# Seven of sixteen blocks of a re-read V half kept in a constant's buffer and in spare PSUM columns, with the first q blocks written by VectorE

## The chip, the cores and the metric

One NeuronCore of a Trainium2 chip runs the whole kernel as one launch. TensorE (PE) multiplies, VectorE (DVE), ScalarE (ACT) and GpSimd (POOL) do the rest, SyncE (SP) issues the loads, and sixteen DMA engines move the bytes from the chip's main memory into on-chip memory (SBUF); matmul results land in PSUM, eight banks of 512 float32 columns per partition. The metric is the device time of one execution in microseconds (us). The kernel before took 178.01 us (median of 3 runs, 177.15 to 178.4).

## The reference

Four tokens (batch 4, one position, width 512) go through attention, a gated MLP, the same attention and the same MLP again, each with a layer norm before it and a residual after it. Attention looks at the last W = 2048 of 8192 cached positions; 32 query heads share 8 key/value heads.

```python
x = x + attn(layernorm(x)); x = x + mlp(layernorm(x))   # twice, with the same weights and caches
# attn: q = x @ wq; p = softmax(q k^T * Dh**-0.5) over 2048 keys; o = p v; o @ wo
# mlp:  (sigmoid(x @ w_gate) * (x @ w_up)) @ w_down,   512 -> 1792 -> 512
```

In bfloat16 one pass over the keys is 16 MB (4 batches, 8 heads, 2048 keys, 128 values) and one over the values as much again. wq and wo are 4 MB each, the three MLP matrices 1.75 MB each.

## The kernel before, in words

**Stages.** The first q projection, attention over heads 0 to 7 (`attn_first`), the MLP (`glu`, k = 0), the second q projection (`q_second`), attention over heads 7 to 0 (`attn_second`, whose steps are called 2.0 to 2.7; step 2.0 is head 7), the MLP again (k = 1).

**Memory and loads.** SBUF is one `arena` of 50 slots of 4 KB per partition and a smaller tensor `side` of scratch. All K blocks stay in the arena from the first pass to the second. V does not fit, so it is loaded twice, but for a few blocks: some stay in the arena, and some wait in PSUM banks that are idle between the passes. VectorE puts them there with `transpose` (`stash`, line 578, and `stash_half`, line 600) and takes them back (line 593 in `load_stash`, line 606 in `unstash_half`). A "tile" is two slots: for head h and batch pair bp, 64 partitions for each of two batches, 32 keys on each, so that a half tile (one slot) is 16 key blocks of 128 values. Tile (6, 0) is kept by half: its second half stays where it was (`KEPT`), its first half is loaded again as `("Vh", 0, 6, 0, 1)`, 512 KB.

**Places.** Between the passes the weights of the first MLP and of the second q projection are loaded into half tiles. Each is given its place by name in the source: `Y`, `Z` and `GA` are the tiles of V (7, 0), (7, 1) and (6, 0), `WQ` is the first tile of wq, `SP` is `side`. `homes` holds the place of each load, `hfree` the halves that are free by then, `give` frees one by hand, `done` frees what was read for the last time. A load waits for the last reader of its place; SP issues the loads in the written order, so a load that waits holds back all behind it (line 401 issues every load).

**Order of work.** Each operation is recorded with what it reads and writes (`P.op`). A planner (`_schedule`) then runs through all of them with estimated durations and gives each engine a fixed order; `_assign_sync` puts in the semaphore waits. From the first MLP on, TensorE's order is the written order (`P.chain = True`).

**The second q projection and the first two scores.** wq is used in two halves: half 1 feeds heads 4 to 7 and is multiplied first (`q_mms(1, 1, ...)`, line 828), `q_turn` transposes the result on VectorE (line 840, named qt) and scales it into `qh` (line 844, qc). For each score step TensorE then spreads one head's q into a block form with four matmuls against shifted identities (`qx`, line 875) and ScalarE copies that to `qbd` (`qe`, line 880). The score (`softmax_unit`) is first four matmuls that write the mask (M, line 905) and then sixteen with q and K (S, line 916). In step 2.0 the matmuls of wq block (1, 0) stand between M and S (argument `between`). After the scores VectorE takes the maximum (mx, line 929). Each score frees its K slots for loads of V:

```python
qx(0)
score(0, lambda: q_mms(1, 0, OBS[1], (1,)))
qx(1)
score(1)
turn(0)
```

`permo` (128 x 512, bfloat16) is a constant, a permutation that VectorE writes at the start (line 705). TensorE reads it once per step of the first attention (`pm`, line 1024) and then not again until step 2.7.

Of the kernel before, what the change touches and what calls it, by code (L numbers as in the profile page):

```python
# [6 lines left out]
F32 = mybir.dt.float32  # L7
# [271 lines left out]
def build(nc, A_x, A_k, A_v, A_wq, A_wo, B_wg, B_wu, B_wd, out, cfg=None):  # L279
# [45 lines left out]
    with es:  # L325
# [90 lines left out]

        homes = {}
# [71 lines left out]
        def load_half(name, src, rate, size, where_):  # L489
            left[name] = 1  # L490
            homes[name] = [where_]
            on_free[name] = lambda s: hfree.add(s)

            def emit(s):
                dma(str(name), slot_ap(s)[:, 0:size], src, w=stok(s, size), rate=rate)
            loads.append((name, emit))
# [25 lines left out]
        def load_wq(k):  # L522
# [3 lines left out]
            else:  # L526
                for i in (1, 0):
                    for c in range(i, NC):
                        load_half(("wq", c, k, i), wq_d[:, c, i * SLOT:(i + 1) * SLOT], "bw_4k", SLOT,
                                  (((Y, 0), (Y, 1), (WQ, 1), (WQ, 0)), (None, (WQ, 0), (GA, 0), (SP, 0)))[i][c])  # L530
# [23 lines left out]
        def load_glu(k):  # L554
            for nm, src, two in (("wg", wg_d, wg_p), ("wu", wu_d, wu_p)):
                if k == 0:
                    for c in range(NC):
                        load_half((nm, c, k), src[:, c, :], "bw_3k", F,
                                  (((WQ, 0), (GA, 0), (SP, 0), (Y, 0)), ((Y, 1), (Z, 0), (WQ, 0), (GA, 0)))[nm == "wu"][c])
# [3 lines left out]
            for n, (a, b) in enumerate(bounds_of(k)):  # L563
                if k == 0:
                    load_half(("wd", a, k), wd_d[:, a:b, :].rearrange("p k n -> p (k n)"), "bw_4k", (b - a) * D,
                              ((SP, 0), (Y, 0), (Y, 1), (Z, 0))[n])
# [42 lines left out]
        def load_v(h, bp, k, n_use):  # L609
            name = ("V", h, bp, k)  # L610
            tiles = {(HKV - 2, 0): ((GA, 0),), (HKV - 3, 1): ((Y, 0), (Y, 1))}.get((h, bp)) if k else None
            if tiles is not None:
                halves[h, bp] = []
                for n, tile in enumerate(tiles):
                    half = ("Vh", n, h, bp, k)
                    load_half(half, pair_d(A_v, h, bp)[:, :, n * SLOT:(n + 1) * SLOT], "bw_4k", SLOT, tile)
                    halves[h, bp].append((half, 0))
                if len(tiles) == 1:
                    halves[h, bp].append((KEPT, 0))
                return  # L620
# [5 lines left out]
        def keep_half(s):  # L626
            hfree.add(s)
            where[KEPT] = s + 1
            left[KEPT] = 2
        on_free[GA] = keep_half  # L630
# [205 lines left out]
        def q_turn(k, i, qb, buf=None, toks=(("e", 0), ("e", 1)), after=()):  # L836
# [4 lines left out]
                 r=[("qrow", i)], w=toks, banks=(qb,), after=after)  # L841
            qi = qh[:, i * 64:(i + 1) * 64]
# [14 lines left out]
        def q_second(variance):  # L857
# [3 lines left out]
            q_mms(1, 1, WB, (2, 3))  # L861
            q_mms(1, 0, OBS[1], (0,))
            fresh.append(q_turn(1, 1, WB))
# [28 lines left out]
        late = {}  # L892

        def softmax_unit(tag, hk, wait=False, q=True, between=None):
# [3 lines left out]
            bank, pt = {HKV: (OBS[0], 2), HKV + 1: (WB, 3)}.get(u, (SB[k2], k2))  # L898
# [3 lines left out]
            def e_m(pe):  # L902
                last = None
                for gi in range(4):
                    last = pe.matmul(ps[32 * gi:32 * gi + 32, bank, :], msk_s[:, :],  # L905
                                     msk_m[:, :].unsqueeze(1).broadcast_to([128, 256, 2]), start=True, stop=False)
                return last

            def e_s(pe):
# [664 lines left out]
```

## Time and profile before

| what | value |
|---|---|
| median of 3 runs (range) | 178.01 us (177.15 to 178.4) |
| the profiled execution's own time | 177.0 us |
| its span, first to last instruction | 175.3 us |
| busy: PE, DVE, ACT, POOL | 105.7, 104.4, 32.7, 22.2 us |
| bytes by DMA | 70.00 MB, mean 399 GB/s |
| first attention ends, first MLP (last wo matmul to the residual) | 104.8 us, 118.5 us |
| second attention, from the first score to the residual | 124.6 to 163.0 us |

The page is one execution. "Busy" is time in which an engine executed; the idle time of an engine that does not bound the kernel costs nothing. The DMA rows are the engines' busy share in tenths and the GB/s moved, in 40 slices of 4.38 us. An "issue" is SP's instruction that starts a load; a load is done ("lands") when all sixteen engines have finished their shares. The clock that the profile grants to TensorE is 1.00 until 157 us and 0.50 after.

### The profile page before, as it was taken

Reading aid. Unit: us, or ns where it says so; the run is one execution under the profiler, and the core shown is the slowest. Engines: PE = TensorE matmul, PEld = TensorE weight load, DVE = VectorE, ACT = ScalarE, POOL = GpSimd, SP = SyncE. Lnnn points to the kernel's source line nnn. Section 1 sums busy time; section 2 is a strip of 40 time slices with the busy share of each in tenths; the row PEclk is TensorE's granted clock in tenths of the full one; section 3 lists DMA queues with packets and bytes.
Section 4 is the critical chain, followed back from the end, with each engine's and each line's share of the span. In section 5 each row is a group of like instructions: output and inputs, shape, how many; then the busy total and the mean of one; then the engine's idle time right before and its main releaser. Section 6 shows DMA issues by size and latency. Waiting matters only on the chain.

```text
span 175.3 us, 3927 instructions
## 1 busy us (share of the span) xinstructions
PE 105.7 (60%) x1661; PEld 54.7 (31%) x1661; DVE 104.4 (60%) x257; ACT 32.7 (19%) x87; POOL 22.2 (13%) x90
## 2 busy tenths in 40 slices
PE   0536246259566273661765456547977999776673
PEld 0203112014334041340445452142322444445321
DVE  6307997994957738378322381316299999751351
ACT  2002031322303003021030000100143455430011
POOL 6100010101101001010010000000011453442000
PEclk9999999999999999999999999999999999995555
DMA  5999999999999999999999999999999999999980
GB/s 188 426 426 426 426 419 424 408 421 423 419 419 412 420 424 426 421 405 427 419 419 415 415 400 407 402 410 403 394 413 404 423 419 424 421 416 423 419 344 25
DMA packets 12226, 70.00 MB, mean 399 GB/s; under 512 B 1320, under 2 KB 1328, under 8 KB 6064
## 3 DMA queue, kind: packets, MB, share of 16 engines
q1 hardware_dynamic: 12200, 69.74, 97.1%
q8 instruction: 13, 0.21, 0.5%
q14 instruction: 5, 0.04, 0.1%
q10 hardware_dynamic: 8, 0.00, 0.0%
HBM read 69.73 MB, written 0.00 MB: 398 GB/s over the span
## 4 chain that ended last, share of the span: by engine, by line
DMA 52%; DVE 24%; PE 19%; issue 2%; SPq 1%; ACT 0%; DVEq 0%
DMA arena<-in_A_v_cache_dram 20%; DMA arena<-in_B_w_down_dram 18%; DVE arena L887 12%; DMA arena<-in_A_wq_dram 10%; PE ps L916 8%; DMA arena<-in_B_w_gate_dram 5%; DVE small L929 3%; PE ps L905 3%; PE ps L1088 2%; DVE small L933 1%; DVE arena L593 1%; PE ps L1006 1%; DVE side L937 1%; PE ps L828 1%; DVE small L941 1%
## 5 line engine op out<-in xcount | busy, mean ns | idle before, releaser
L887 DVE STREAM_TRANSPOSE arena<-arena 128x1024 f32<-128x1024 f32 x32 | 37.0, 1205 | 0.1
L1006 PE MATMUL ps<-side,arena 128*128 128x8 bf16 x576 | 18.2, 168 | 14.1 <-DMA arena<-in_A_v_cache_dram 14.0
L916 PE MATMUL ps<-arena,side 128*32 128x512 bf16 x256 | 25.0, 524 | 0.1
L1006 PEld LDWEIGHTS ps<-side,arena 128*128 128x128 bf16 x576 | 16.7, 104 | 20.5 <-DMA arena<-in_A_v_cache_dram 18.8
L929 DVE TENSOR_REDUCE small<-ps 128x1 f32<-128x512 f32 x16 | 10.8, 676 | 17.6 <-PE ps L916 17.5
L944 ACT ACTIVATE side<-ps,small 128x512 bf16<-128x512 f32 x16 | 11.0, 687 | 36.8 <-PE ps L1024 18.3
L905 PE MATMUL ps<-small,msk_s 128*32 128x512 bf16 x64 | 8.4, 512 | 13.9 <-DVE arena L887 13.1
L880 ACT CAST side<-ps 128x256 bf16<-128x256 f32 x16 | 5.9, 370 | 34.4 <-PE ps L916 25.4
L959 ACT CAST side<-ps 128x512 bf16<-128x512 f32 x16 | 9.4, 586 | 10.8 <-PE ps L957 10.8
L916 PEld LDWEIGHTS ps<-arena,side 128*32 128x32 bf16 x256 | 8.2, 119 | 10.0 <-issue 7.2
L973 POOL CAST small<-small 128x1 bf16<-128x1 f32 x9 | 1.7, 188 | 76.1 <-ACT side L944 76.1
L957 PE MATMUL ps<-side,perm 128*128 128x512 bf16 x16 | 7.9, 494 | 5.2 <-ACT side L944 5.2
L828 PE MATMUL ps<-arena,xn 128*4 128x512 bf16 x60 | 7.5, 572 | 3.9 <-DMA arena<-in_A_wq_dram 3.6
L784 ACT ACTIVATE small<-ps 128x4 f32<-128x4 f32 x4 | 0.7, 174 | 48.1 <-PE ps L780 48.1
L1379 PE MATMUL ps<-arena,xn 128*4 128x448 bf16 x60 | 7.2, 549 | 3.3 <-DMA arena<-in_B_w_up_dram 1.5
L964 DVE STREAM_TRANSPOSE side<-side 128x256 f32<-128x256 f32 x16 | 6.9, 433 | 2.0 <-ACT side L959 1.8
L875 PE MATMUL ps<-side,eyew 32*128 32x64 bf16 x64 | 5.6, 217 | 3.4 <-ACT side L880 2.4
L1088 PE MATMUL ps<-arena,side 128*32 128x512 bf16 x112 | 7.3, 381 | 0.2 <-DVE small L941 0.2
L1014 DVE TENSOR_TENSOR onb<-ps,rinv 128x16 bf16<-128x16 f32 x9 | 1.7, 185 | 9.0 <-PE ps L1006 8.8
L905 PEld LDWEIGHTS ps<-small,msk_s 128*32 128x32 bf16 x64 | 1.7, 97 | 16.8 <-DVE arena L887 15.4
L1388 DVE STREAM_TRANSPOSE side<-ps 128x448 f32<-128x448 f32 x4 | 2.6, 650 | 7.3 <-PE ps L1379 7.3
L840 DVE STREAM_TRANSPOSE side<-ps 128x512 f32<-128x512 f32 x3 | 2.1, 716 | 7.9 <-PE ps L828 7.8
(123 smaller groups left out, 137.8 us busy)
## 6 DMA issues: line engine op xcount, KB each, us to landing
arena<-in_A_v_cache_dram SPq DMA_DIRECT2D x27, 1024.0 KB, 18.8
arena<-in_A_k_cache_dram SPq DMA_DIRECT2D x16, 1024.0 KB, 24.9
arena<-in_A_wq_dram SPq DMA_DIRECT2D x4, 1024.0 KB, 7.8
arena<-in_A_wo_dram SPq DMA_DIRECT2D x3, 1024.0 KB, 26.5
arena<-in_A_wq_dram SPq DMA_DIRECT2D x6, 512.0 KB, 6.3
arena<-in_B_w_up_dram SPq DMA_DIRECT2D x4, 448.0 KB, 6.1
arena<-in_B_w_gate_dram SPq DMA_DIRECT2D x2, 896.0 KB, 21.7
arena<-in_B_w_up_dram SPq DMA_DIRECT2D x2, 896.0 KB, 23.9
```

What stands on the lines that cost most here:

```text
L828: last = pe.matmul(ps[32 * hh:32 * hh + NB, qb, :], xn[:, c * NB:(c + 1) * NB], src[:, o + hh * 512:o + (hh + 1) * 512], start=(c == 0), s ...
L887: P.op("vector", "T%d_%d" % (h, t), c_dve(1024), lambda v, v32=v32: v.transpose(v32, v32), r=[("slot", 4 * h + t)], w=[("slot", 4 * h + t)])
L905: last = pe.matmul(ps[32 * gi:32 * gi + 32, bank, :], msk_s[:, :], msk_m[:, :].unsqueeze(1).broadcast_to([128, 256, 2]), start=True, stop= ...
L916: last = pe.matmul(ps[32 * gi:32 * gi + 32, bank, :], qbd[:, q0:q0 + 32], kt[:, cp // 2, cp % 2, jh * NJ:(jh + 1) * NJ, :], start=False, s ...
L929: lambda v: v.tensor_reduce(nmax[:, k2:k2 + 1], ps[:, bank, :], AXX, ALU.max),
L944: lambda a: a.activation(prow[:, :].rearrange("p (m x t) -> p m x t", x=32, t=2), ps[:, bank, :].rearrange("p (m t x) -> p m x t", x=32, t ...
L957: lambda pe: pe.matmul(ps[:, pb, :], perm[:, :], prow[:, :], start=True, stop=True),
L959: P.op("scalar", "pc" + tag, c_act(512), lambda a: a.copy(prow[:, :], ps[:, pb, :]), r=[("ppb", pb)], w=[("prow",)], banks=(pb,))
L964: P.op("vector", "pt" + tag, c_dve(256), lambda v: v.transpose(et, prow[:, :].bitcast(F32)), r=[("prow",)], w=[("e", k2)])
L1006: last = pe.matmul(ps[:, ob, bp * 8:bp * 8 + 8], src[:, j * 128:(j + 1) * 128], ev[:, j % 2, j % 16 // 2, x0:x0 + 8], start=(j == 0), stop ...
L1088: last = pe.matmul(ps[32 * g:32 * g + 32, ob, :], ew[:, g, mq, t], src.rearrange("p (m t d) -> p t m d", t=2, d=128)[:, t], start=(n == 0) ...
L1379: last = pe.matmul(ps[32 * g:32 * g + NB, gub[n], 0:NF], xn[:, c * NB:(c + 1) * NB], src[:, g * NF:(g + 1) * NF], start=(c == 0), stop=(c ...
```

## The change

1. The load of the first half of tile (6, 0) leaves out its first 896 elements per partition (7 of the 16 key blocks): 128 x 1152 instead of 128 x 2048 elements.
2. Those seven blocks are kept from the first pass. Four (512 elements) are copied by ScalarE into `permo` (`save_half`, sv0) after its last use of the first attention; three (384 elements, as 192 float32) are transposed by VectorE into columns 304 to 495 of PSUM bank 7 (sv1). The half that held them is given back only then.
3. `restore_half` copies them back beside the new load: ScalarE (rv0), VectorE (rv1); GpSimd then writes `permo` anew in four instructions.
4. The loads between the passes are dealt to other places, and the reloaded halves too.
5. The q blocks of steps 2.0 and 2.1 are no longer made by qx and qe. GpSimd clears `qbd` (qz), and VectorE writes the blocks straight from qt's result, four instructions a step (`q_block`).
6. The masks of both steps are written earlier (`mask_unit`), and the score of step 2.0 is cut into two parts of eight matmuls, with the wq matmuls between them.

```diff
-                dma(str(name), slot_ap(s)[:, 0:size], src, w=stok(s, size), rate=rate)
+                o = dma(str(name), slot_ap(s)[:, skip:size], src[:, :, skip:] if skip else src, w=stok(s, size), rate=rate)
+                if skip:
+                    late["saved_deps"] = set(o.deps)
...
-                                  (((Y, 0), (Y, 1), (WQ, 1), (WQ, 0)), (None, (WQ, 0), (GA, 0), (SP, 0)))[i][c])
+                                  (((Y, 1), (GA, 0), (WQ, 1), (WQ, 0)), (None, (WQ, 0), (Y, 0), (SP, 0)))[i][c])
...
-                                  (((WQ, 0), (GA, 0), (SP, 0), (Y, 0)), ((Y, 1), (Z, 0), (WQ, 0), (GA, 0)))[nm == "wu"][c])
+                                  (((WQ, 0), (SP, 0), (Y, 0), (Y, 1)), ((Z, 0), (GA, 0), (WQ, 0), (Y, 0)))[nm == "wu"][c])
...
-                              ((SP, 0), (Y, 0), (Y, 1), (Z, 0))[n])
+                              ((SP, 0), (Y, 1), (Z, 0), (GA, 0))[n])
...
-            tiles = {(HKV - 2, 0): ((GA, 0),), (HKV - 3, 1): ((Y, 0), (Y, 1))}.get((h, bp)) if k else None
+            tiles = {(HKV - 2, 0): ((Y, 0),), (HKV - 3, 1): ((Y, 1), (GA, 0))}.get((h, bp)) if k else None
...
         def keep_half(s):
-            hfree.add(s)
             where[KEPT] = s + 1
             left[KEPT] = 2
+            P.op("vector", "sv1", c_dve(SAVED_P), lambda v: v.transpose(saved_p, saved_f(s)),
+                 r=[("slot", s)], w=[("sv", 1)], banks=(CB,))
+
+        SAVED_S, SAVED_P = REP * 128, 192
+        SAVED = SAVED_S + 2 * SAVED_P
+        saved_p = ps[:, CB, 304:304 + SAVED_P]
+
+        def save_half():
+            s = base[GA]
+            P.op("scalar", "sv0", c_act(SAVED_S), lambda a: a.copy(permo[:, :], slot_ap(s)[:, 0:SAVED_S]),
+                 r=[("slot", s)], w=[("permo",)])
+            give(s)
+
+        def restore_half():
+            s = need(late["saved"])
+            a = P.op("scalar", "rv0", c_act(SAVED_S), lambda a: a.copy(slot_ap(s)[:, 0:SAVED_S], permo[:, :]),
+                     r=[("permo",)], w=[("rv", 0)], after=tuple(fresh))
+            b = P.op("vector", "rv1", c_dve(SAVED_P), lambda v: v.transpose(saved_f(s), saved_p),
+                     r=[("sv", 1)], w=[("rv", 1)], banks=(CB,), after=tuple(fresh))
+            for o in (a, b):
+                o.deps.update(late["saved_deps"])
+            for m in range(REP):
+                P.op("gpsimd", "permo2%d" % m, 300.0,
+                     lambda g, m=m: g.affine_select(permo[:, m * 128:(m + 1) * 128].rearrange("p (r v) -> p r v", r=REP),
...
             q_mms(1, 1, WB, (2, 3))
+            P.op("gpsimd", "qz", 600.0, lambda g: g.memset(qbd[:], 0.0), w=[("q", k2) for k2 in range(2)])
+            mask_unit("2.0", HKV)
             q_mms(1, 0, OBS[1], (0,))
-            fresh.append(q_turn(1, 1, WB))
+
+            def blocks(buf, toks):
+                for k2 in range(2):
+                    q_block(HKV - 1 - k2, k2, buf, toks)
+            fresh.append(q_turn(1, 1, WB, blocks=blocks))
+            mask_unit("2.1", HKV + 1)
+
+        def q_block(h, k2, buf, toks):
+            p0 = h % 4 * 32
+            for a in range(4):
+                P.op("vector", "qb%d_%d" % (h, a), c_dve(64),
+                     lambda v, a=a: v.tensor_tensor(
+                         qbd[32 * a:32 * a + 32, k2 * 256:(k2 + 1) * 256].rearrange("p (c b a r) -> p c b a r", c=4, b=NB, a=4)[:, :, :, a, :],
+                         buf[p0:p0 + 32, :].rearrange("p (r c y) -> p c y r", c=4, y=32)[:, :, 0:NB],
+                         lnr[p0:p0 + 32, 0:NB].unsqueeze(1).unsqueeze(3).broadcast_to([32, 4, NB, REP]), ALU.mult),
+                     r=toks + [("lnr", 0), ("q", k2)], w=[("qa", k2, a)])
...
+            early = HKV <= u < HKV + 2
+            if wait and not early:
+                mask_unit(tag, u)
+            rd = [("msk_s",), ("msk_m",)] + [("slot", 4 * hk + t) for t in range(4)] + [("q", k2)]
+            if early:
+                rd += [("qa", k2, a) for a in range(4)]
+            if between is not None:
+                P.op("tensor", "Sa" + tag, 8 * tm["pe_row"], lambda pe: e_s(pe, (0, 1)), r=rd, w=[("pss", pt)], banks=(bank,))
+                between()
+                P.op("tensor", "S" + tag, 8 * tm["pe_row"], lambda pe: e_s(pe, (2, 3)), r=rd, w=[("pss", pt)], banks=(bank,))
...
                     give(base[Z])
+                    save_half()
...
-            qx(0)
+            restore_half()
             score(0, lambda: q_mms(1, 0, OBS[1], (1,)))
-            qx(1)
             score(1)
```

## The prediction, made before the changed kernel was run

> **What bounds the kernel now.** I read the page first: the DMA rows, then the chain that ended last.
>
> ```profile
> span 175.3 us, 3927 instructions
> ...
> DMA  5999999999999999999999999999999999999980
> GB/s 188 426 426 426 426 419 424 408 421 423 419 419 412 420 424 426 421 405 427 419 419 415 415 400 407 402 410 403 394 413 404 423 419 424 421 416 423 419 344 25
> ...
> q1 hardware_dynamic: 12200, 69.74, 97.1%
> ...
> DMA 52%; DVE 24%; PE 19%; issue 2%; SPq 1%; ACT 0%; DVEq 0%
> ```
>
> The DMA engines are busy in every slice but the first and the last two, and the loads' queue takes 97.1% of sixteen engines. So a byte that is not moved is worth its time, as long as (a) the queue never runs dry and (b) the computing that follows the last loads keeps up. The chain in order of time gives the price of (a):
>
> ```profile
> 0.79 0.42 SPq L401
> ...
> 2.19 10.86 DMA arena<-in_A_wq_dram
> ...
> 146.35 25.46 DMA arena<-in_B_w_down_dram
> ```
>
> The first four loads are 1 MB each, issued from 0.79 us; the fourth lands at 13.05. At 421 GB/s a megabyte takes 2.49 us, so the first landed at 13.05 - 3 x 2.49 = 5.58, 4.8 us after its issue to an empty queue. A load therefore needs about 4.8 us from issue to landing for 1 MB, 3.5 for 512 KB (1.25 less), 3.4 for 448 KB; issued earlier than that before its turn, it waits behind others and nothing is lost. At the end one of the last loads waits 25 us in the queue: there the queue is deep. It is shallow between the passes, where the issue rows give 6.1 to 6.3 us for weight halves and 5.7 for the three V halves. For (b), the timeline of the last microseconds:
>
> ```profile
> 169.79 0.22 DVE L1406 TENSOR_TENSOR rinv<-side,onp 128x56 bf16<-128x56 f32 x1
> 170.64 1.02 PE L1420 MATMUL ps<-arena,rinv 128*4 128x128 bf16 x32 [1.15 <-DMA arena<-in_B_w_down_dram]
> 171.86 1.01 PE L1420 MATMUL ps<-arena,rinv 128*4 128x128 bf16 x24 [0.20 <-DMA arena<-in_B_w_down_dram]
> ```
>
> The last MLP's input is ready at 170.01, its weights at 170.64: computing has 0.63 us to spare, no more. From 126.6 to 157 it is engine work almost without a gap (VectorE 11.2 of 12 us from 134 to 146), so what starts late at 126.6 ends late at 170. With x the shift of the second attention's first maximum, the time changes by the larger of minus the DMA saving and x - 0.63.
>
> **Part 1, the bytes.** 128 rows x 1,792 bytes = 0.229 MB less. Loads in 4 KB rows run at 402 to 409 GB/s (the stretches of 2 us from 110 to 122 us): 0.56 us. The new load has rows of 2.3 KB; the stretches with the 2 KB rows of wo and the 3.5 KB rows of the MLP, 100 to 104 us, give 392 to 396 GB/s. 0.295 MB at 0.395 is 0.75 us against 0.524 MB at 0.41, 1.28: **0.53 saved** (0.50 to 0.56).
>
> **Parts 2 and 3, keeping the blocks.** Saving three blocks (sv1, 128x192): no such row; between 0.2 (the smallest operations) and 0.43 (256 columns, L964), I take 0.35. VectorE idles 4.9 us before 99.20, waiting for V; it goes there. Saving four (sv0) is a ScalarE copy like L959's 0.59 (128x512) and starts when `pm` is through with the constant at 103.71, so ends by 104.4; ScalarE idles 18.5 us there. The load that waits for it stands in SP's queue behind one that waits for the last PSUM stash (L600) until 104.83 anyway. Hidden by 0.4 us. Restoring: rv0 0.59 on ScalarE, idle before the first exponential at 128.25; rv1 0.35 on VectorE before 126.62; four GpSimd selections of 0.29 (L643, the same shape), 1.2 us, done by about 127.7, while GpSimd's next work came at 130.30. The restored half is read by the value product of step 2.1 after 136. Nothing on the path; if ScalarE's copy slipped behind the exponential, the price would be its 0.59.
>
> **Part 4, the places.** SP is in order, so each later wait counts for all behind it. The first w_up waits for the last stash instead of the one before: issue 104.9 instead of 102.70, landing due at 109.9. The fourth waits for the third w_gate's reader: 108.3 instead of 107.2, due 113.3. wq block (1, 0) waits for the last w_down matmul: 118.4 instead of 117.5, due 124.2. That leaves 5.0, 5.0 and 5.9 us against 3.4 to 3.5 needed: no loss on the engine that ends last. Engines that run ahead may idle a little, which costs nothing while another is later.
>
> **Parts 5 and 6, the first scores.** Here the waits decide. The timelines of TensorE and of VectorE:
>
> ```profile
> 121.65 0.60 PE L828 MATMUL ps<-side,xn 128*4 128x512 bf16 x4
> 122.96 0.60 PE L828 MATMUL ps<-arena,xn 128*4 128x512 bf16 x4 [0.72 <-DMA arena<-in_A_wq_dram]
> 123.52 0.36 PE L875 MATMUL ps<-side,eyew 32*128 32x64 bf16 x4
> 123.82 0.62 PE L905 MATMUL ps<-small,msk_s 128*32 128x512 bf16 x4
> 124.25 0.61 PE L828 MATMUL ps<-arena,xn 128*4 128x512 bf16 x4
> 124.64 1.93 PE L916 MATMUL ps<-arena,side 128*32 128x512 bf16 x16
> ...
> 127.36 1.10 PE L916 MATMUL ps<-arena,side 128*32 128x512 bf16 x16
> ```
>
> ```profile
> 122.30 0.72 DVE L840 STREAM_TRANSPOSE side<-ps 128x512 f32<-128x512 f32 x1 [0.68 <-PE ps L828]
> 123.12 0.26 DVE L844 TENSOR_TENSOR side<-side,small 128x64 bf16<-128x64 f32 x1
> 126.62 0.69 DVE L929 TENSOR_REDUCE small<-ps 128x1 f32<-128x512 f32 x1 [3.24 <-PE ps L916]
> ```
>
> Now: the first mask goes into the 0.72 us gap (122.25 to 122.87), wq block (0, 0) runs at 122.96 as before, the second mask until 124.18. VectorE writes head 7's four blocks from 123.12. The nearest row is L844, 0.26 for the same 64 elements and the same operation: 4 x 0.26 ends at 124.16 (at 0.17, the smallest such operation, 123.8). GpSimd's clearing of `qbd`, 0.53 (L650), starts when the wq block in `side` has been read, 122.3, and ends with the transpose. So the first half score starts at 124.2; at the slow pace (1.73 for 16) 0.87, then wq block (1, 0) 0.60 (landed 124.2), then the second half 0.87: end 126.54 against 126.57 now. **x is -0.05.** Behind it VectorE still has head 6's blocks, qc and rv1: 5 x 0.26 + 0.35 after 124.16 is 125.8, inside the 3.24 us of idling that the last line shows, with 0.8 to spare. The second score follows at once, without its qx and mask: end 128.3 or earlier, against 128.46. What is late next: the third V half waits for wq block (1, 0), which now stands behind the first half score: issue 125.7 instead of 124.9. It landed at 130.5 and is due at 130.0 now: 4.3 us against 3.5. The next loads wait for the two scores: 126.6 as before, then 0.2 earlier, due at 132.5 and 135 against 4.8 needed. It holds, by 0.8 us.
>
> The sum: DMA -0.53, computing x - 0.63 = -0.68; the larger is -0.53. I take 0.05 off for the short lead. **177.0 - 0.5 = 176.5 by the profiled execution's own time; the runs shown had a median 1.0 above it, so 177.5 by that measure.**
>
> **Rivals.**
> A. *Saved, but lost to an empty queue.* Transfers end 0.5 us earlier while the loads that follow are issued no earlier. The stretches of 2 us show that it is tight already:
>
> ```profile
> 122.00:124.00 2.00, 1.28 (x16) 0.43 (x12) 0.98 (x2) 0.07 (x1) 0.00 (x0) 1.00 1.05 406
> 124.00:126.00 2.00, 2.00 (x24) 0.67 (x20) 0.00 (x0) 0.30 (x1) 0.00 (x0) 1.00 0.97 371
> 126.00:128.00 2.00, 1.87 (x28) 0.67 (x24) 1.24 (x4) 0.37 (x1) 0.00 (x0) 1.00 1.01 408
> ```
>
> 371 instead of 407 GB/s for 2 us is 0.18 us. If the third half's lead were short by all 0.8 us that it is later, the loss would eat the gain: change 0 to -0.2, 178.0. Against: 4.3 is more than 3.5.
> B. *Slower: head 7's blocks on VectorE.* They stand on the path where ScalarE's copy was hidden behind the mask. With q us each the half score starts at 123.12 + 4q, x = 4q - 1.1, and the kernel is slower once x is over 0.63: q over 0.43. At 0.6 it is x = 1.3 and +0.7: 178.7. For: the output is scattered in runs of four. Against: L844 reads the same pattern and takes 0.26.
> C. *Faster: TensorE at full pace earlier.* Sixteen score matmuls took 1.93 us from 124.64 and 1.10 from 127.36, so TensorE changed pace at about 126.5, after some 3.5 us without a gap. The mask in the gap makes that run start at 119.7 instead of 122.96. If the pace comes before 124.2, the scores end 0.9 us earlier, x = -0.9; the loads behind them too, and the dip above goes: -0.53 - 0.2 to -0.4, 177.2. The Trainium skill, page "TensorE: Matmul & The Clock Gate", section "What's actually happening", says that the clock is let go after about 3.4 us of sustained activity in a free-running window; the 3.5 us of the trace agree, and by that rule this rival is the forecast.
> D. *The load doesn't shrink.* Its access is written as 128 x 1152; nothing speaks for this.
>
> **Numbers.** Forecast 0.55, A 0.17, B 0.1, C 0.16, 0.02 for what I don't see. The runs before spread over 1.25 us, so each case's time carries some 0.6 us to both sides: from C less 0.6 to a little above B, **176.5 to 178.9**. A measurement of this kernel tells about 1%, 1.8 us, from no change: faster by that needs C and a low draw (0.07), slower needs q near 0.9 or a stall that I don't see (0.08), within 1% 0.85.
>
> **What would show it.** The V half's row at 288 KB and some 69.77 MB in all; the four block writes at 0.2 to 0.3 us with the half score at 124.2 (q and x); the first maximum at 126.5; the stretch 124 to 126 us near 371 GB/s or above (below it, A); the last w_down matmuls still released by their load (otherwise x has eaten the 0.63). A median off by over 0.7 us with all these as foretold would mean that the spread between executions is larger than the change.

## The result

Over 22 runs each, on the same chip, the kernel after has a median of 178.68 us (177.07 to 179.65), the kernel before 177.53 (177.0 to 178.4). The ratio is **1.006, with an interval of 1.0041 to 1.0078: slower by 1.1 us** where 0.5 us faster was forecast. A second series gave 1.004 (1.0017 to 1.0063). A few executions of the runs below fell into a slower state of the chip, and ratios, medians and means leave them out. The profiled execution of the kernel after took 178.84 us, its span 177.0.

The page of the kernel after, its span, the GB/s of the 40 slices, the loads' queue and the chain that ended last:

```profile
span 177.0 us, 3929 instructions
...
GB/s 180 429 418 431 424 418 422 406 429 418 418 420 414 421 420 420 418 410 427 422 415 415 412 402 394 386 410 404 355 292 409 426 424 416 426 412 425 412 340 23
...
q1 hardware_dynamic: 12200, 69.51, 96.4%
...
DMA 51%; DVE 26%; PE 19%; issue 2%; SPq 1%; DVEq 0%; ACT 0%
```

69.51 MB instead of 69.74 came through the queue, so the bytes are gone. The chain that ended last is still half DMA. But the queue's share of the span fell, from 97.1% to 96.4%, by more than the bytes (0.3%), and there are two slices, 355 and 292 GB/s, where 394 and 413 stood before. In stretches of 2 us (busy time by engine, granted clock, DMA share, GB/s), kernel after:

```profile
126.00:128.00 2.00, 2.00 (x24) 0.76 (x19) 1.24 (x5) 0.62 (x1) 0.37 (x2) 1.00 0.93 340
128.00:130.00 2.00, 0.99 (x16) 0.30 (x8) 1.86 (x7) 0.46 (x1) 0.87 (x3) 1.00 0.77 223
130.00:132.00 2.00, 1.25 (x17) 0.47 (x21) 2.00 (x5) 1.18 (x4) 0.40 (x3) 1.00 1.03 311
```

Before, the first of these stretches moved 408 GB/s, the other two 414:

```profile
128.00:130.00 2.00, 1.37 (x21) 0.36 (x13) 2.00 (x5) 1.27 (x4) 0.00 (x0) 1.00 1.06 414
130.00:132.00 2.00, 1.56 (x27) 0.55 (x22) 1.86 (x6) 0.37 (x2) 0.71 (x3) 1.00 0.99 414
```

The missing 362 GB/s over 2 us are 0.72 MB, at 414 some 1.7 us: three times the 0.23 MB that are saved. TensorE's timeline of the kernel after shows where the lateness begins (start, duration, what it does, idle time before it and its releaser):

```profile
121.45 0.59 PE L861 MATMUL ps<-arena,xn 128*4 128x512 bf16 x4
122.73 0.60 PE L861 MATMUL ps<-side,xn 128*4 128x512 bf16 x4 [0.69 <-DMA side<-in_A_wq_dram]
123.11 0.64 PE L950 MATMUL ps<-small,msk_s 128*32 128x512 bf16 x4
124.00 0.60 PE L861 MATMUL ps<-arena,xn 128*4 128x512 bf16 x4 [0.24 <-DMA arena<-in_A_wq_dram]
124.38 0.64 PE L950 MATMUL ps<-small,msk_s 128*32 128x512 bf16 x4
125.49 1.05 PE L974 MATMUL ps<-arena,side 128*32 128x512 bf16 x8 [0.47 <-DVE side L911]
126.30 0.67 PE L861 MATMUL ps<-arena,xn 128*4 128x512 bf16 x4
```

The last wq block of half 1, in `side`, is multiplied at 122.73 instead of 121.65, and TensorE idles 0.69 us for its load; before, that load landed at 121.60, while TensorE still worked on the block ahead of it. Everything behind is late by as much, and VectorE's timeline adds a little:

```profile
123.38 0.72 DVE L873 STREAM_TRANSPOSE side<-ps 128x512 f32<-128x512 f32 x1 [1.62 <-PE ps L861]
124.23 2.25 DVE L911 TENSOR_TENSOR side<-side,small 32x64 bf16<-32x64 f32 x8
126.52 0.26 DVE L879 TENSOR_TENSOR side<-side,small 128x64 bf16<-128x64 f32 x1
126.81 0.38 DVE L653 STREAM_TRANSPOSE arena<-ps 128x192 f32<-128x192 f32 x1
127.86 0.69 DVE L992 TENSOR_REDUCE small<-ps 128x1 f32<-128x512 f32 x1 [0.67 <-PE ps L974]
```

A block write takes 0.28. The first maximum comes at 127.86 instead of 126.62: 1.08 of this 1.24 are there already at qt (123.38 against 122.30), only 0.16 is the new way of making the blocks. The end is still released by the last loads, which now land 1.8 us later:

```profile
172.37 1.02 PE L1484 MATMUL ps<-arena,rinv 128*4 128x128 bf16 x32 [1.14 <-DMA arena<-in_B_w_down_dram]
173.61 1.02 PE L1484 MATMUL ps<-arena,rinv 128*4 128x128 bf16 x24 [0.22 <-DMA arena<-in_B_w_down_dram]
```

### The profile page after: what moved, and what is told of

Same layout as the page of the kernel before. It is cut to its first block, busy times and chain, and to the rows that moved or that the text cites. A ratio compares the mean times of both kernels' runs of the same rounds, so it can differ in the third digit from the quotient of the medians.

```text
span 177.0 us, 3929 instructions
## 1 busy us (share of the span) xinstructions
PE 105.7 (60%) x1653; PEld 54.6 (31%) x1653; DVE 107.2 (61%) x267; ACT 33.2 (19%) x87; POOL 24.0 (14%) x95
## 3 DMA queue, kind: packets, MB, share of 16 engines
q1 hardware_dynamic: 12200, 69.51, 96.4%
HBM read 69.51 MB, written 0.00 MB: 393 GB/s over the span
## 4 chain that ended last, share of the span: by engine, by line
DMA 51%; DVE 26%; PE 19%; issue 2%; SPq 1%; DVEq 0%; ACT 0%
DMA arena<-in_A_v_cache_dram 19%; DMA arena<-in_B_w_down_dram 14%; DVE arena L939 12%; PE ps L974 9%; DMA arena<-in_A_wq_dram 6%; DMA side<-in_A_wq_dram 4%; DMA arena<-in_B_w_gate_dram 4%; DVE small L992 3%; DMA arena<-in_B_w_up_dram 3%; PE ps L950 3%; PE ps L1151 2%; DVE small L996 1%; DVE arena L596 1%; PE ps L1069 1%; DVE side L1000 1%
## 5 line engine op out<-in xcount | busy, mean ns | idle before, releaser
L932 ACT CAST side<-ps 128x256 bf16<-128x256 f32 x14 | 5.2, 370 | 29.4 <-PE ps L974 25.4
L927 PE MATMUL ps<-side,eyew 32*128 32x64 bf16 x56 | 4.8, 215 | 3.3 <-ACT side L932 2.4
```

## The experiments

All in one table. "Steps" are worked out from the landing marks in the trace of the profiled execution: sixteen DMA engines report each load, and a step is the time from the last mark of one load to the last mark of the next, here for wq blocks (2, 1) and (3, 1), the second and third load of wq between the passes; undisturbed it is 1.25 to 1.29 for 512 KB. "Spread" is last mark less the mean of the sixteen, for the load before these.

| kernel | ratio to before (interval) | medians, it and before | spread | steps |
|---|---|---|---|---|
| before | 1 | | 0.88 | 1.25, 1.27 |
| after | 1.006 (1.0041 to 1.0078) | 178.68, 177.53 | 0.59 | 2.18, 1.28 |
| after, second series | 1.004 (1.0017 to 1.0063) | 178.19, 177.31 | 0.60 | 1.47, 1.27 |
| parts 5 and 6 undone | 1.0041 (1.0015 to 1.0067) | 178.12, 177.44 | 0.69 | 1.58, 1.13 |
| the same, second series | 1.0026 (0.9998 to 1.0054) | 178.05, 177.31 | 0.57 | 1.61, 1.29 |
| parts 5 and 6 alone | 1.0007 (0.998 to 1.0033) | 177.51, 177.44 | 0.79 | 1.25, 1.52 |
| wq (1, 0) ahead of the score | 1.0016 (0.9984 to 1.0048) | 177.89, 177.44 | 0.48 | 1.83, 1.28 |
| the same, second series | 1.0036 (1.0011 to 1.0062) | 178.05, 177.31 | 0.72 | 1.68, 1.28 |
| new places alone | 1.0013 (0.998 to 1.0046) | 177.66, 177.44 | 0.61 | 1.65, 1.13 |
| the same, second series | 1.0034 (1.0011 to 1.0056) | 177.76, 177.38 | 0.54 | 1.83, 1.29 |
| bytes left out here | 0.999 (0.997 to 1.0011) | 177.41, 177.29 | 0.82 | 1.29, 1.27 |
| bytes left out late | 0.9974 (0.9947 to 1.0001) | 176.68, 177.29 | 0.91 | 1.27, 1.33 |
| small load last | 1.0021 (0.9989 to 1.0053) | 178.00, 177.29 | 0.40 | 2.60, 1.28 |
| small load last, old q blocks | 1.0032 (1.0005 to 1.0059) | 178.08, 177.29 | 0.59 | 2.38, 1.27 |
| three blocks, old places | 0.9994 (0.9971 to 1.0016) | 177.09, 177.38 | 0.84 | 1.25, 1.28 |
| new places, fetches moved | 1.0101 (1.0074 to 1.0128) | 179.31, 177.38 | 0.48 | 1.28, 1.28 |
| three late blocks | 0.998 (0.9959 to 1.0001) | 177.10, 177.38 | 0.83 | 1.28, 1.28 |

Single executions of one changed kernel lie 0.6 to 2.6 us apart, so an interval of twelve runs is some 0.5% wide (that with the fetches moved has six), and the verdicts lean on several kernels with one property, and on the traces. The diffs are shortened: `...` stands for what is left out, a semicolon joins two lines, and remarks behind `#` are not in the code.

**Three theories: the third V half, the places, one DMA engine.** The first theory, T1, was read off the kernel after: its third V half was issued at 127.00 instead of 124.91, since its place is freed by the matmuls of wq block (1, 0), which stand behind the first half score. T2 blames the new places, T3 an accident of one DMA engine.

Parts 5 and 6 undone:

```diff
-            P.op("gpsimd", "qz", ...); mask_unit("2.0", HKV)
-            fresh.append(q_turn(1, 1, WB, blocks=blocks)); mask_unit("2.1", HKV + 1)
+            fresh.append(q_turn(1, 1, WB))
...
+            qx(0)
             restore_half()
             score(0, lambda: q_mms(1, 0, OBS[1], (1,)))     # one score of 16 matmuls, behind the wq matmuls
+            qx(1)
```

> The kernel after with parts 5 and 6 undone: the blocks of steps 2.0 and 2.1 are made by qx and qe again, the masks stand before their scores, the score of step 2.0 is whole and behind the matmuls of wq block (1, 0). The saved 0.229 MB and the new places stay. T1 (the loss is the third V half's place, which comes free behind VectorE's blocks and the first half score): the third half's issue is back at 124.9 to 125.3 and the saving shows: 0.5 us faster than before, ratio 0.997. T2 (the loss is the new places): 0.5 to 1 us slower than before, ratio 1.004, as the kernel after. T3 (an accident of one DMA engine beside an instruction fetch, which the profile of the kernel after shows at 118.8 us): with other instructions the fetches fall elsewhere, so about 0.5 faster too, but the profile of T1's other kernels (parts 5 and 6 alone) would not be slower.

Slower by 0.4%. The third half's issue went back to 125.28, as T1 said, and the time did not follow.

Parts 5 and 6 alone, in the kernel before:

```diff
+            P.op("gpsimd", "qz", ...); mask_unit("2.0", HKV)
-            fresh.append(q_turn(1, 1, WB))
+            fresh.append(q_turn(1, 1, WB, blocks=blocks)); mask_unit("2.1", HKV + 1)
...
-            qx(0)
             score(0, lambda: q_mms(1, 0, OBS[1], (1,)))     # split, as in the kernel after
-            qx(1)
```

> The kernel before with parts 5 and 6 alone: blocks by VectorE, masks early, split score; nothing saved, all places old. T1: the third half is issued 0.8 to 1 us later than before with nothing gained elsewhere, and the queue runs dry by 0.6 to 1.2 us: 0.6 to 1.2 slower than before, ratio 1.004 to 1.007. T2: the same as before within 0.3 us. T3: the same as before, unless its own fetches happen to fall badly.

No difference, though the third half was issued at 126.34, 1.4 later than before. As the cause of the whole loss T1 falls here: the wait that the theory blames is there, and its price, a ratio of 1.004 or more, lies outside the interval.

The kernel after with wq block (1, 0) ahead of the score:

```diff
             if between is not None:
-                P.op("tensor", "Sa" + tag, ..., lambda pe: e_s(pe, (0, 1)), ...)
                 between()
-                P.op("tensor", "S" + tag, ..., lambda pe: e_s(pe, (2, 3)), ...)
-            else:
-                P.op("tensor", "S" + tag, ..., e_s, ...)
+            P.op("tensor", "S" + tag, ..., e_s, ...)
```

> The kernel after, but the matmuls of wq block (1, 0) stand ahead of the whole score of step 2.0, as in the kernel before; blocks by VectorE and early masks stay. T1: the third half's place no longer waits for VectorE, its issue is at about 124.9 to 125.3, the saving shows in part: 0.2 to 0.5 us faster than before, ratio 0.998, so 1.3 to 1.6 less than the kernel after. T2 and T3: no change against the kernel after, 0.8 to 1.2 slower than before, ratio 1.006.

Not faster than before, 1.0016: T1 missed again; the interval could not tell it from the kernel after.

New places alone, in the kernel before (part 4 of the diff and nothing else):

> The kernel before with the new places alone; nothing saved, q blocks and scores as before. T1: no change, within 0.2 us of before, ratio 1.000. T2: 0.6 to 1 us slower, ratio 1.004 to 1.006. T3: no change.

1.0013 with a wide interval: neither theory is settled by the time. The trace says more. In this kernel too TensorE waits for the block in `side`, and the step of the block ahead of it is 1.65 where the kernel before and the one with parts 5 and 6 alone have 1.25. TensorE's timeline, new places alone:

```profile
121.06 0.60 PE L828 MATMUL ps<-arena,xn 128*4 128x512 bf16 x4
121.84 0.60 PE L828 MATMUL ps<-side,xn 128*4 128x512 bf16 x4 [0.17 <-DMA side<-in_A_wq_dram]
```

**What are the bytes worth, and does the order of the V loads matter?** Two kernels leave bytes out and change nothing else.

```diff
-                    load_half(half, pair_d(A_v, h, bp)[...], "bw_4k", SLOT, tile)
+                    load_half(half, pair_d(A_v, h, bp)[...], "bw_4k", SLOT, tile, 896 if len(tiles) == 1 else 0)
```

> The kernel before, and nothing changed but the load of the first half of V tile (6, 0): it leaves out the first 896 elements of each partition (0.229 MB), and nothing puts them back, so the output lacks these seven key blocks. The pure worth of the bytes at their place. Forecast of the prediction (a byte is worth its time wherever it is saved): 0.5 us faster than before, ratio 0.997. Empty queue (the loads behind it are issued when computing frees their places, so bytes that are saved ahead of the gap at 128 us only make the gap longer): no change, 0 to 0.15 us faster, ratio 0.999 to 1.000; the mean landing of V tile (5, 0), three loads later, is where it was within 0.15 us.

```diff
-            load(name, n_use, "bw_8k", (2 * SLOT, pair_d(A_v, h, bp), True))
+            load(name, n_use, "bw_8k", (2 * SLOT, pair_d(A_v, h, bp), True), 896 if k and (h, bp) == (0, 0) else 0)
```

> The kernel before, and nothing changed but the last load of V, tile (0, 0) of the second attention: it leaves out the first 896 elements of each partition, so the same 0.229 MB behind the gap, where the queue is 19 us deep; the output lacks these key blocks. Empty queue: here the bytes are worth their time, 0.5 us faster, ratio 0.997. If computing bounds the end instead (the last MLP's input is ready only 0.63 us ahead of its weights): up to 0.5 faster still, as 0.63 is more than 0.5. If neither kernel of this pair is faster, the time isn't bound by bytes at all and lies in how the sixteen engines lag behind each other.

The same 0.229 MB gave 0.1% at the first place (between 0.3% faster and 0.1% slower) and 0.26% at the second (between 0.5% faster and none). On one chip the medians of the two are 0.73 us apart, the means only 0.42, which is as much as their uncertainty. So the times make it likely that the place matters, but do not settle it, and the forecast's 0.997 is the edge of the first interval. The mean of the sixteen landing marks, one execution each, shows where the bytes go:

| kernel | V (6, 0), first half | V (5, 0), three loads on | last w_down |
|---|---|---|---|
| before | 127.41 | 132.61 | 171.02 |
| bytes left out here | 126.97 | 132.60 | 171.32 |
| bytes left out late | 127.56 | 132.88 | 171.00 |
| after | 127.14 | 134.04 | 172.56 |

Here the load lands 0.44 earlier, and three loads on nothing is left of it. From that landing of V (5, 0) to the last column it takes 38.12 us with the late bytes left out, 38.20 in the kernel with three late blocks below, and 38.40 to 38.80 in the other fifteen profiles: the late bytes do shorten what is behind them. The stretches of the kernel with the bytes left out here:

```profile
124.00:126.00 2.00, 2.00 (x21) 0.72 (x24) 0.00 (x0) 0.37 (x1) 0.00 (x0) 1.00 1.02 388
126.00:128.00 2.00, 2.00 (x24) 0.60 (x20) 1.16 (x4) 0.37 (x1) 0.00 (x0) 1.00 0.93 358
128.00:130.00 2.00, 2.00 (x25) 0.55 (x21) 1.97 (x5) 1.05 (x3) 0.00 (x0) 1.00 1.06 360
```

358 and 360 where before has 408 and 414: 104 GB/s over 2 us, 0.21 MB, of which the stretch ahead had made good 0.03 (388 against 371). The DMA share beside it stays at 1.06 from 128 to 130 us, since it counts a packet's whole time, and 8 KB packets that began there lasted up to 1.25 us instead of 0.31. The saved bytes came back as a hole in the queue, since the loads behind are issued when computing frees their places, and not a moment earlier.

The small load last, in the kernel with wq (1, 0) ahead and in the one with the old q blocks:

```diff
-            tiles = {(HKV - 2, 0): ((Y, 0),), (HKV - 3, 1): ((Y, 1), (GA, 0))}.get((h, bp)) if k else None
+            tiles = {(HKV - 2, 0): ((GA, 0),), (HKV - 3, 1): ((Y, 0), (Y, 1))}.get((h, bp)) if k else None
...
                     if n_v == 2:
+                        loads.append(loads.pop(-3))
```

> The kernel with wq block (1, 0) ahead of the first score again (as in the run of that name), and besides the three V loads between the passes in another order: the two 512 KB halves of tile (5, 1) first, into the places that come free first, and the small load of tile (6, 0), 288 KB, last, into the place of wq block (1, 0); its blocks are put back behind that. Nothing is left out. Empty queue: each large half is issued one place earlier, 121.7 and 124, and the load that is issued last, at 125.3, is the one that needs the shortest lead; the gap at 128 us closes for the most part and the saving shows: 0.3 to 0.5 us faster than before, ratio 0.997 to 0.998, and 0.5 to 0.8 less than the run with only wq block (1, 0) moved. If the order of these loads plays no part: 0.2 to 0.4 slower than before, as that run.

> The same order of the three V loads in the kernel with the old way of making the q blocks (saving and new places kept). Empty queue: 0.2 to 0.4 us faster than before, ratio 0.998, so 0.9 less than the run with the old q blocks and the order of the kernel after. If the loss of that run was the places or the lag of single DMA engines, it stays: 0.5 to 0.7 slower than before.

Both missed: 1.0021 and 1.0032. The order was as written, but in both profiles the lag of the wq block was the largest of all, and the whole chain started late. TensorE's timeline, small load last:

```profile
121.75 0.59 PE L861 MATMUL ps<-arena,xn 128*4 128x512 bf16 x4 [0.52 <-DMA arena<-in_A_wq_dram]
123.02 0.60 PE L861 MATMUL ps<-side,xn 128*4 128x512 bf16 x4 [0.68 <-DMA side<-in_A_wq_dram]
```

By then every kernel with the new places had a lag at wq block (2, 1). Of the four with the old ones only that with parts 5 and 6 alone had one, 0.25 us and a load later. The marks show its form. In the run with the small load last, fifteen engines have finished wq block (2, 1) by 120.37 and the sixteenth at 121.70; in the kernel after 120.50 and 121.41; in the kernel before 120.15 and 120.33. At 118.1 to 118.8 one 16 KB packet of the instruction queue passes in each of them, for 1.0 to 1.05 us. One packet is on one DMA engine, and one engine is what lags.

**Is it the places, is it the fetch, and can the idea be saved?**

Three blocks kept by VectorE alone, with the old places: `permo` is not used, the half is free at 99 us, and no load has to move.

```diff
         def keep_half(s):
-            hfree.add(s)
             where[KEPT] = s + 1
             left[KEPT] = 2
+            P.op("vector", "sv1", ..., lambda v: v.transpose(saved_p, saved_f(s)), ...)
+            hfree.add(s)
```

> Saving with the old places: only the three blocks that VectorE keeps in PSUM are saved (0.098 MB less in the load of the first half of tile (6, 0)), permo isn't used, so the half comes free at 99 us and every load between the passes keeps its place of before; q blocks and scores as before; nothing is left out. If the new places make the loss (all six profiles of kernels with them show one DMA engine 0.3 to 1.3 us behind the others at the load of wq block (2, 1) of the first half, none of the four with the old places does): that load's step stays at 1.25 to 1.3 us, and the time is that of before within 0.2 us, as saved bytes at this spot gave nothing. If keeping and putting back makes it (sv1, rv1): 0.4 to 0.7 slower, as with the old q blocks and new places.

0.9994, and no lag: both steps are undisturbed. TensorE's timeline:

```profile
121.18 0.60 PE L848 MATMUL ps<-arena,xn 128*4 128x512 bf16 x4
121.69 0.60 PE L848 MATMUL ps<-side,xn 128*4 128x512 bf16 x4
122.98 0.60 PE L848 MATMUL ps<-arena,xn 128*4 128x512 bf16 x4 [0.68 <-DMA arena<-in_A_wq_dram]
```

VectorE's keeping and putting back shows no cost here, nor does a saving that leaves the places alone. It shows no gain either, though the interval of 0.2 to 0.3% to both sides is wider than what 0.098 MB could give.

New places with the instruction fetches moved (80 idle matmuls at the start):

```diff
+            def e_shift(t):
+                for _ in range(80):
+                    last = t.matmul(ps[0:4, WB, 0:4], ident[:, 0:4], ident[:, 0:4], start=True, stop=True)
+            P.op("tensor", "shift", 2000.0, e_shift, ...)
```

> The kernel before with the new places alone, and besides 80 idle 4x4 matmuls on TensorE at 3 us, whose result is overwritten. They move every later fetch of 256 TensorE instructions forward in the program by 160 instructions: the fetch at 118.4 us comes at about 107 to 108, that of 103 at 97. If the lag is the fetch on a DMA engine that the shorter lead has robbed of its advance: at 107 the load behind takes it up, the step of wq block (2, 1) falls from 1.6 to 2.4 us to under 1.35, and the time is 0.3 to 0.7 less than that of the new places alone. If it isn't the fetch: the lag stays at that load, and the time is the same as with the new places alone within 0.3.

> The kernel before with the new places alone, once more, beside the run with the moved fetches. New places as the cause: 0.3 to 0.9 us slower than before in the mean, and the lag of one engine at the load of wq block (2, 1) again. If its 0.6 in the first run was chance: within 0.2 of before.

The new places alone were slower again, 1.0034, with the lag. With the fetches moved, the packet of 118.4 passed at 105.5, and the step of wq block (2, 1) fell to 1.28 as foretold. But the time did not fall, it rose to 1.0101. The next fetch had moved forward too, from 132.4 to 121.26, and the lag was now at the load that passed then, wq block (0, 0), whose step went from 1.27 to 2.46. TensorE's timeline:

```profile
121.71 0.60 PE L834 MATMUL ps<-side,xn 128*4 128x512 bf16 x4
124.17 0.59 PE L834 MATMUL ps<-arena,xn 128*4 128x512 bf16 x4 [1.86 <-DMA arena<-in_A_wq_dram]
```

So the lag goes where the fetch goes; that half of the expectation held. The other half, 0.3 to 0.7 us less, did not. In the profiled execution 1.0 us of the price lies behind the span, where a fourteenth fetch falls; without that the ratio would be some 1.0045 (an estimate), no lower than that of the places alone.

Three late blocks: the kernel before, with three blocks of the last V tile kept in PSUM.

```diff
+        def save_late(s):
+            P.op("vector", "sv", ..., lambda v: v.transpose(saved_p, tile_ap(s)[:, 0:384].bitcast(F32)), ...)
+            pool.release(s)
+        on_free["V", 0, 0, 0] = save_late
...
+            load(name, n_use, "bw_8k", (2 * SLOT, pair_d(A_v, h, bp), True), 384 if k and (h, bp) == (0, 0) else 0)
```

> A version that may beat both: the kernel before, and three blocks of the last V tile, (0, 0), are kept from the first pass in PSUM columns 320 to 511 of bank 7 by VectorE (0.35 us at 40 us, where VectorE waits for loads) and put back by it at about 140 us (0.35 us); its second load is 0.098 MB smaller, where the queue is 19 us deep. Places, q blocks and scores as before; nothing is left out. By the late bytes of the earlier run: 0.24 us faster, ratio 0.9986. If VectorE's 0.35 in the second attention counts: the last MLP's input is 0.35 later, its weights 0.24 earlier, of the 0.63 to spare 0.04 are left, still 0.24. If the time isn't bound by late bytes: same or up to 0.35 slower.

0.998 (0.9959 to 1.0001), 0.3 us: the lowest ratio of the kernels that leave nothing out, against 1.004 and 1.006 of the kernel after. All twelve runs lie between 176.93 and 177.55. That it beats the kernel before is likely, with an interval that just touches no change. In its profile the end is no longer released by a load:

```profile
171.17 1.63 PE L1441 MATMUL ps<-arena,rinv 128*4 128x128 bf16 x56 [0.67 <-DVE rinv L1427]
```

The first of the weights had landed at 170.62, so here a larger saving would show only with less computing.

**The share of the third half.** The kernel after and two variants once more, on one chip.

> The kernel after, unchanged, beside the two runs below on one chip. Places alone gave ratios of 1.001 and 1.003. If the third V half, which waits in the kernel after for VectorE's blocks and the first half score, costs time of its own: 0.9 to 1.1 us slower than before, ratio 1.005 to 1.006, and 0.5 or more over both runs below. If it costs nothing beside the places: 0.4 to 0.7 slower, the same as they within 0.3.

> The kernel after with wq block (1, 0) ahead of the first score, once more. Third half as a cause of its own: 0.3 to 0.5 us slower than before, ratio 1.002 to 1.003, what the places make. No part of it: 0.4 to 0.7 slower, as the kernel after.

> The kernel after with parts 5 and 6 undone, once more. Third half as a cause of its own: 0.3 to 0.6 slower than before, ratio 1.002 to 1.004, as the places alone, and 0.4 or more under the kernel after. No part of it: the same as the kernel after within 0.3.

1.004, 1.0036 and 1.0026: all three slower, and not to be told apart. In the profiles the third half was issued at 126.31, 125.26 and 125.34. That wait is real, and it reaches a later load: the mean landing of V (5, 0) is 133.28 to 134.07 in the six profiles whose third half was issued after 126 us, among them both of the kernel after and that of parts 5 and 6 alone, and 132.60 to 133.10 in the other eleven. What it costs in time stays open. By the means of both series, weighted by their scatter, the kernel after is 0.27 us above these two variants (-0.06 to 0.61) and 0.47 above the places alone (0.08 to 0.87), while parts 5 and 6 alone took the time of the kernel before.

## Why the prediction was wrong, step by step

**"So a byte that is not moved is worth its time", -0.53.** This step failed first. Its condition (a), a queue that never runs dry, did not hold at the spot: the load stands just ahead of the shallow stretch, and where its bytes are left out they come back as a hole of 0.21 MB. The times, 0.999 here and 0.9974 late, agree, but their intervals overlap. Rival A had the mechanism and named 371 GB/s as its sign. It was put off with "4.3 is more than 3.5", which is a statement about the engine that ends last. The leading engines, 1.2 to 1.7 ahead by their first marks, had that much less lead, and in the kernel before they already ran dry (between the last two wq loads the first mark steps 1.56 instead of 1.27). Measured in place of -0.53: +0.1 by the medians and -0.2 by the means of the run with the bytes left out here (-0.5 to +0.2).

**Part 4, "no loss on the engine that ends last. Engines that run ahead may idle a little, which costs nothing while another is later".** The leads were as worked out: 4.98, 4.98 and, with the lag in it, 6.74 against 5.0, 5.0 and 5.9. The last engine indeed lost nothing, and the leading ones idled. Both can be seen in the run with the small load last, where it is largest, against the one with the bytes left out here: the first mark of the four loads from the fourth w_up on is 111.64, 112.79, 114.41, 115.82 instead of 111.55, 112.53, 113.81, 115.09, the last mark of the fourth 116.84 instead of 116.90. In all eleven profiles with the new places that first mark is at 115.37 to 115.82, in the six with the old ones at 115.05 to 115.13, with last marks of 116.76 to 117.00 in both. What failed is "costs nothing". The advance is a reserve. With it, an instruction packet at 118 us can be taken up by an engine that is ahead: spread 0.79 to 0.91 in the six profiles with the old places, and over the two steps 0 to 0.1 us are lost in five of them, 0.23 in the sixth (parts 5 and 6 alone). Without it, spread 0.40 to 0.72 in the ten with the new places and unmoved fetches, and 0.2 to 1.3 us are lost (0.6 in the mean, counted from 2 x 1.27). And these loads are ones that computing waits for, so the issues behind them are late too (in the second series of the places alone V (5, 0) is issued at 127.24 instead of 126.62). In time, the new places alone cost 0.22 and 0.38 us by the medians of the two series, 0.27 and 0.44 by the means.

How the lag comes about can be read from the sorted marks of one load and of the next. In each of these sixteen profiles one engine falls back while the packet passes, by 1.34 to 1.43 us with the old places and 1.40 to 1.71 with the new ones, and the load is late by what the engine's advance on the last one does not cover: 1.55 less 0.64 is the 0.91 of the kernel after, 1.52 less 0.19 the 1.33 of the small load last, and in the kernel before 1.46 of advance cover 1.34. With the old places that advance was 1.17 to 1.46, with the new ones 0.19 to 1.39.

The Trainium skill, page "Runtime: NRT & Kernel Launch", section "Instruction fetch mechanics", says that an engine's instructions come in blocks of 16 KB, 256 of them, over a DMA queue, and that crossing a block is mostly hidden. The trace agrees on the size (13 packets, 0.21 MB) and on the count (258 of TensorE's recorded matmuls and weight loads from one to the next on average). For the DMA engines, which bound this kernel, a fetch is not hidden: it takes 0.9 to 1.4 us of one of them each.

That the places are the cause of a loss is shown by the kernels with them together (ratios of 1.0013 to 1.0041 beside the kernel after) and by the three blocks kept without them. That the lag follows the fetch is shown; so it is no accident, as T3 had it, though its size differs from one execution to the next. That the lag makes the 0.2 to 0.45 us is only argued, and the traces speak in part against it: single executions with a lag ended at 177.08 and 176.78, and in the six profiles with a lag of 0.3 to 0.6 us and a third half issued by 125.6 V (5, 0) landed at 132.73 to 132.90, no later than with the old places. The end belongs to whichever engine is last then: the last mark of the last w_down load lies 0.8 to 2.0 us behind the mean of its sixteen.

**Parts 2 and 3, hidden.** Right: 0.39 and 0.38 for VectorE's two transposes, 0.62 for each of ScalarE's copies, 1.44 on GpSimd, none of them waited for by the scores or by a load; for VectorE's two the run with three blocks and the old places shows it in time.

**Parts 5 and 6, x = -0.05** (126.54 against 126.57 is -0.03). The price of a block was right, 0.28 against 0.26, so rival B did not come. By its own step x was 0.16: the first half score began 0.14 after the fourth block and took 1.05, not 0.87. The rest of the 1.24 is the late load. "Issue 125.7" for the third half was 127.00 and 126.31 for the same two reasons, and "it holds, by 0.8 us" fell with it; but parts 5 and 6 on the old places showed no cost (1.0007).

**Rival C, full pace earlier.** It did not come. The first eight score matmuls took 1.05 us, 131 ns each, no faster than before (1.93 for sixteen, 121 each). The early masks do not close TensorE's gaps, because the late loads (0.69 and 0.24 in the timeline above) and then VectorE's blocks (0.47) make new ones. Four score matmuls follow each other in 0.42 us until 128.0 and in 0.22 from 128.3 on; in the kernel before the pace changes at about 126.9. The Trainium skill, page "TensorE: Matmul & The Clock Gate", section "What's actually happening", asks for sustained activity of some 3.4 us. In the trace of the kernel after the pace changes some 2.7 us after the end of the last gap, at 125.49, so a gap of 0.47 us did not start the count anew.

**The sum.** Forecast -0.53, measured +1.1 and +0.7 by the ratios of the two series. Of the difference, 1.2 to 1.6, the lost saving is 0.35 to 0.65 and the places are 0.2 to 0.45. That leaves 0.1 to 1.05. The kernel after stands 0.47 us above the places alone, just clear of the noise, so parts 5 and 6 with the late third half, on top of the places, probably hold some of the rest; which of them, and by what way, stays open.

## What to carry to other kernels

Before counting a saved byte, find the next place behind it where the loads are issued by computing and not by the queue: ahead of such a place the byte only lengthened the hole here, and behind the last one it probably gave time (0.9974 and 0.998, each interval just touching no change). Look at all sixteen landing marks of a load and not only at the last: the engines that ran ahead were the reserve that took up instruction fetches, and a later issue that cost the last engine nothing still used part of that reserve up. Do not accept a change by its largest part; here the part that was thought free, the dealing of places, cost 0.2 to 0.45 us, and the saved bytes that were worked out at 0.53 gave 0.2 at most by the medians and means.

## What was not expected of the hardware

- An instruction fetch of TensorE is one 16 KB packet on one DMA engine, for 0.9 to 1.1 us at 118 us. It comes at the same place of TensorE's program in each kernel, so some 160 TensorE instructions (80 matmuls with their weight loads) at 3 us moved it from 118.4 to 105.5 and the next from 132.4 to 121.3 us.
- The fetches are what drives the sixteen engines apart while the queue is deep. In the kernel before all marks of a load lie within 0.41 us until the first fetch at 30.5 us; of the next load one engine is 1.92 behind the first and the others are within 0.40. By the load that lands from 101.06 us on, six such fetches and two 8 KB packets of another instruction queue have passed, and six engines are 1.50 to 1.90 behind, two 0.83 and 1.16, the other eight within 0.41. The trace does not name the engine of a packet, but these marks fit another engine each time. Where the queue runs dry the engines come together: by the load ahead of wq block (1, 1) the marks lie within 1.7 us in the kernel before and within 1.0 in the run with the small load last.
- The row of the granted clock can show full clock where the trace has no entry. In the kernel before the first entry is at 126.9 us. Sixteen score matmuls at 51 us took 1.92 us there, under a row that says full clock, and 1.93 in the second series with wq (1, 0) ahead, whose row says half from 47 to 126 us; at 127 us sixteen took 1.10 in the kernel before. So the 1.00 that the page of the kernel before shows up to 126.9 is not the pace that TensorE ran at.
